# Attention handed to the scheduler: its hand-written order dropped, the first group's early matmuls at the lowest priority

## The chip, the core and the metric

One core of a Trainium2 chip runs the kernel. The metric is the time of one execution on the device in microseconds (us), the median of several runs. The engines are named as the profile names them: PE (matrix multiply, with PEld for its weight loads), DVE (vector), ACT (activation), POOL (GpSimd) and SP, which only issues transfers here. Each engine works through its own instructions strictly in the order in which they stand in the program; an instruction that waits for another engine holds up everything behind it on its own engine.

## The reference

```python
B, H, Sl, D = 4, 8, 512, 64;  Sg = 32;  window = 32;  scale = 1 / sqrt(D)
k_all, v_all = concat(k_g, k_l), concat(v_g, v_l)          # along the sequence
out_g = softmax(scale * q_g @ k_all.T) @ v_all             # 32 global queries see all
s_ll  = where(|i - j| <= window, scale * q_l @ k_l.T, -1e9)
s_l   = concat(scale * q_l @ k_g.T, s_ll)                  # local queries: globals and a band
out_l = softmax(s_l) @ v_all
x = concat(out_g, out_l) as 2176 tokens x 512
x = (silu(x @ w_gate) * (x @ w_val)) @ w_out               # 512 -> 1536 -> 512
y = mish(x @ w_in) @ w_out2                                # 512 -> 2048 -> 512
```

The seven arrays of the two feed-forward layers are wide numbers of 8 bytes, which the kernel turns into a high and a low 32-bit half itself.

## The kernel before

**Attention.** The 32 heads of the four batches are worked as 16 head pairs, numbered 0 to 15, four to a batch. `att_hp` is a head pair's work in seven steps: transpose keys and queries (`qkT`, L195); scores of the local rows in two halves (`sc`, L238, half 0 and half 1), each with a masked minimum on DVE (L243, four times) and an exponential on ACT (L247, four times); a reciprocal of the row sums (L226, L227 on DVE) and the multiplication with it on POOL (L228, L230); the transposes of the two halves (`pT`, L195) with a copy on ACT (L265); and the output (`o`, L272 and L276), which `split_to_x` writes as a high and a low half into the token tiles `x0` to `x4` (L137 on ACT, L138 on DVE). The halves' reciprocals are made by `normalise`: that of half 0 is written behind the scores of half 1.

`att_g` is the same for the 32 global queries, once for two head pairs: scores `ga` (L286), minimum on DVE (L294 to L296), exponential on ACT (L297), scaling on DVE (L303), transposes `gT` (L195), output `go` (L320). So a period of the attention is two head pairs with one `ga` in it.

**What goes on beside it.** The first group of the first feed-forward layer (two blocks f of 128 hidden columns) needs six weight blocks, `w0` to `w5`. `w_load` brings one with one transfer of 512 KB on SP's queue into one of three staging buffers `st`; `w_convert` turns it into two halves: a square on ACT (L408, `q<-st`), four operations on DVE (L410 to L414), a copy on ACT (L424), a subtraction on POOL (L425). A staging buffer is free for the next load when L414 is done.

`fill(t)` then works this group for a whole token tile: for both blocks 12 matmuls for `g` and 12 for `v` (L539; `g` and `v` each sum over four blocks kd of the tile, three matmuls each), the gate on ACT and DVE (L544 to L547), the high and low half (L473 on ACT, L459 on POOL), and 24 matmuls for the output (L560) with a copy on DVE (L562). That is 72 matmuls for a tile, and 216 for the three tiles 0, 1 and 2. They are called fill matmuls below. Tiles 3 and 4 of this group are worked behind the attention, as the first units of the dense stage (L448).

**What sets the order.** `attention()` gives every step a number, a place on a line on which head pair n begins at 10n; the steps are sorted by it and called. All of it runs under `tc.manual_schedule()`, so instructions stand on every engine in the order of the calls. The six conversions are at 16 to 48, one after about every 6; the fill of tile i is cut at each `yield` into 12 pieces (six matmuls in nearly all), at 44.9 + 40i onwards.

**The dense stage.** Behind the attention stand the units of all other groups, also in an order written by hand; that part is the same in both kernels. PSUM holds three double banks for attention (`ps_pair`) and two banks `ps_mm` for the fill.

Of the kernel before, what the change touches and what calls it, by code (L numbers as in the profile page):

```python
# [21 lines left out]
def tile_attn_moe_moe2(  # L22
# [73 lines left out]
    def setup():  # L96
        nc.gpsimd.memset(ident, 1.0)
        nc.gpsimd.affine_select(out=ident, in_=ident, pattern=[[-1, 128]], compare_op=ALU.is_equal,
                                fill=0.0, base=0, channel_multiplier=1)
        nc.vector.memset(qgbd, 0.0)  # L100
        for t in (vg, vgb):
            nc.vector.memset(t, 0.0)

        nc.gpsimd.memset(mask, 0.0)
        m = mask[:, 0:192]
        nc.gpsimd.affine_select(out=m, in_=m, pattern=[[1, 192]], compare_op=ALU.is_ge,
                                fill=NEG, base=0, channel_multiplier=-1)
        nc.gpsimd.affine_select(out=m, in_=m, pattern=[[-1, 192]], compare_op=ALU.is_ge,
                                fill=NEG, base=64, channel_multiplier=1)

        nc.gpsimd.tensor_copy(mask7, mask)
        nc.gpsimd.memset(mask7[64:96, 128:192], NEG)
        nc.gpsimd.memset(mask7[96:128, 64:128], NEG)
# [35 lines left out]
    def load_glob(b):  # L149
        gk = g_p.tile([128, 2, 128], F32, tag="gkq", name="gkq")  # L150
        for i, src in enumerate((k_g, q_g)):
            for h in range(2):
                (nc.sync if b else nc.scalar).dma_start(out=gk[:, i, 64 * h:64 * h + 64],
                                  in_=src[b].rearrange("(g h) p d -> h g p d", h=2)[h])
        GK[b] = gk

    def load_qk(b, hp):
        hs = slice(2 * hp, 2 * hp + 2)
        qs = qk_p.tile([128, 4, 2, D], F32, tag="qs", name="qs")
        ks = qk_p.tile([128, 4, 2, D], F32, tag="ks", name="ks")  # L160
        for h in range(2):
            nc.sync.dma_start(out=ks[:, :, h], in_=k_l[b, 2 * hp + h].rearrange("(c p) d -> p c d", p=128))
            nc.sync.dma_start(out=qs[:, 0:3, h],
                              in_=q_l[b, 2 * hp + h, SG:SG + 384, :].rearrange("(c p) d -> p c d", p=128))
        nc.sync.dma_start(out=qs[0:96, 3], in_=q_l[b, hs, SG + 384:SL, :].rearrange("h p d -> p h d"))
        nc.sync.dma_start(out=qs[96:128, 3], in_=q_l[b, hs, 0:SG, :].rearrange("h p d -> p h d"))
        QS[b, hp], KS[b, hp] = qs, ks

    def load_vg(b):

        for k in range(4):
            nc.sync.dma_start(out=vg[32 * k:32 * k + 32, k],
                              in_=v_g[b].rearrange("(g h) p d -> h p g d", h=2)[k % 2])

    def load_vgb(b):
        nc.sync.dma_start(out=vgb[96:128], in_=v_g[b].rearrange("h p d -> p h d"))

    def load_v(b, hp):

        hs = slice(2 * hp, 2 * hp + 2)  # L180
        vw = v_p.tile([128, NB, 2, D], F32, tag="vw", name="vw")
        for h in range(2):
            v = v_l[b, 2 * hp + h]
            windows = bass.AP(v.tensor, v.offset, [[D, 128], [64 * D, NB - 1], [1, D]])
            nc.sync.dma_start(out=vw[:, 0:NB - 1, h], in_=windows)
        nc.sync.dma_start(out=vw[0:64, NB - 1], in_=v_l[b, hs, SL - 64:SL, :].rearrange("h p d -> p h d"))
        nc.sync.dma_start(out=vw[64:128, NB - 1], in_=v_l[b, hs, 0:64, :].rearrange("h p d -> p h d"))
        VW[b, hp] = vw
# [151 lines left out]
    def load_at(i, load):  # L340
        if i < B * HP:
            load(i // HP, i % HP)

    def attention():


        steps = []

        def at(times, gen):
            for t in times:  # L350
                steps.append((t, lambda: next(gen)))

        for n in range(B * HP):
            b, hp = divmod(n, HP)
            t = 10 * n
            if hp == 0:
                steps.append((t - 6, lambda b=b: att_glob(b)))
                if b + 1 < B:
                    steps.append((t + 42.5, lambda b=b: load_vg(b + 1)))
                    steps.append((t + 38.7, lambda b=b: load_vgb(b + 1)))  # L360
            at((t - 4.5, t, t + 2.5, t + 5.8, t + 6.5, t + 9, t + 12), att_hp(b, hp))
            if n + 2 < B * HP:
                steps.append((t - 3, lambda n=n: load_at(n + 2, load_qk)))
                steps.append((t + (13 if hp % 2 else 18.5), lambda n=n: load_at(n + 2, load_v)))
            if hp % 2 == 1:
                at((t + 2.1, t + 4, t + 5, t + 8), att_g(b, hp // 2))
        steps.append((-0.5, lambda: load_v(0, 1)))
        steps += [(9.1, load_next), (9.2, load_next), (9.3, load_next)]
        for i, t in enumerate((16, 22, 28, 34, 41, 48)):
            at((t + 0.3, t + 1.8, t + 3.6), itertools.chain(w_convert(converts.pop(0)), iter([0])))  # L370
        for i, t in enumerate(FILL):
            at([44.9 + 40 * i + 10 * (k // 3) + 3 * (k % 3) + (1 if k % 3 == 2 else 0) for k in range(12)],
               itertools.chain(fill(t), iter([0])))
        for _, go in sorted(steps, key=lambda x: x[0]):
            go()

# [75 lines left out]
    def act_tile(tag, n):  # L452
        return act_p.tile([128, 512], F32, tag=tag, name=tag)[:, 0:n]
# [71 lines left out]
    def fill(t):  # L525

        n = TILES[t]
        fs = GROUPS[0][1]
        x = x_tile(t)
        aa = []  # L530
        for f in fs:
            s = act_tile("t", n)
            for kind in "gv":
                (wh, wl), (xh, xl) = W[0, f, kind], x
                p = ps_mm.tile([128, 512], F32, tag="mm", name=kind)[:, 0:n]
                for k in range(KD):
                    d = slice(128 * k, 128 * k + 128)
                    for j, (a, c) in enumerate(((wh, xh), (wh, xl), (wl, xh))):
                        nc.tensor.matmul(p, lhsT=a[:, d], rhs=c[:, k, :],  # L539
                                         start=(k == 0 and j == 0), stop=(k == KD - 1 and j == 2))  # L540
                    if k == 1:
                        yield
                if kind == "g":
                    nc.scalar.activation(out=s, in_=p, func=AF.Tanh, scale=0.5)  # L544
                    nc.vector.scalar_tensor_tensor(s, s, 1.0, p, op0=ALU.add, op1=ALU.mult)
                else:
                    nc.vector.scalar_tensor_tensor(s, s, 0.5, p, op0=ALU.mult, op1=ALU.mult)  # L547
                    a = hi_lo()
                    high(a, s, n)
                    a_low(a, s, n)  # L550
                    aa.append(a)
                yield
        ya = YA[t] = y_tile(t)
        for c in range(KD):
            d = slice(128 * c, 128 * c + 128)
            p = ps_mm.tile([128, 512], F32, tag="mm", name="mm")[:, 0:n]
            for f, (ah, al) in zip(fs, aa):
                wh, wl = W[0, f, "o"]
                for j, (l, r) in enumerate(((wh, ah), (wh, al), (wl, ah))):
                    nc.tensor.matmul(p, lhsT=l[:, d], rhs=r[:, 0:n], start=(f == fs[0] and j == 0),  # L560
                                     stop=(f == fs[-1] and j == 2))
            nc.vector.tensor_copy(ya[:, c * n:c * n + n], p)  # L562
            if c < KD - 1:
                yield

    def out_rows(c0, n):


        parts = [(b * SL + lo, hi - lo, b * S + r) for b in range(B)
                 for lo, hi, r in ((0, SL - SG, 2 * SG), (SL - SG, SL, SG))]  # L570
        parts += [(B * SL + b * SG, SG, b * S) for b in range(B)]
        for at, k, r in parts:
            a, e = max(c0, at), min(c0 + n, at + k)
            if a < e:
                yield a - c0, r + a - at, e - a
# [37 lines left out]
                nc.scalar.activation(out=yh[:, c, :], in_=ya, func=AF.Copy)  # L613
                nc.gpsimd.tensor_tensor(out=yl[:, c, :], in0=ya, in1=yh[:, c, :].bitcast(F32), op=ALU.subtract)

    with tc.manual_schedule():
        load_glob(0)
        load_qk(0, 0)
        setup()
        load_qk(0, 1)  # L620
        load_v(0, 0)
        load_vg(0)
        load_vgb(0)
        attention()
    early.close()
    ps_acc = pool("ps_acc", 4, space=PS)
    ps_at = pool("ps_at", 2, space=PS)
# [11 lines left out]
    with tc.manual_schedule():  # L639
# [12 lines left out]
        at = -1  # L652
        for n in range(6, len(order)):
            at = max(at + 1, last[order[n - 12]] - 1 if n >= 12 else 0, first[order[n]] - 14)
# [36 lines left out]
```

## Time and profile before

| what | value |
|---|---|
| median of 3 runs | 1036.7 us (1036.5 to 1036.8) |
| the profiled execution's own time | 1028.2 us |
| its span in the trace | 1026.1 us |
| PE busy | 951.0 us, 93% of the span |
| DVE, ACT, POOL busy | 584.9, 526.3, 364.5 us |

The span is the time from the first to the last instruction that the trace holds; the profiled execution took 2.1 us more than that, and 8.5 us less than the median. A busy PE is not always PE at full speed: the trace also has the clock that was granted to it.

### The profile page before, as it was taken

To read this page: it belongs to the slowest core of one execution; us is meant where nothing else is said; L and a number is where in the kernel's file an instruction comes from. 1 tells how busy PE (TensorE), PEld (TensorE's weight loads), DVE (VectorE), ACT (ScalarE), POOL (GpSimd) and SP (SyncE) were. 2 spreads that over 40 slices of the span, in tenths; PEclk is the share of its full clock that TensorE was granted. 3 is DMA by queue.
4 is the path that set the end of the run, shared out by engine and by line. 5 is a ranking of instruction groups with operands and counts; after the bars stand their busy time and mean duration, and the time that the engine had idled before them with its cause. 6 is when DMAs were issued, how large, how long until landed. Compare 5 with 4: busy or idle time off the path is not lost.

```text
span 1026.1 us, 15729 instructions
## 1 busy us (share of the span) xinstructions
PE 951.0 (93%) x6008; PEld 830.1 (81%) x6008; DVE 584.9 (57%) x1097; ACT 526.3 (51%) x1058; POOL 364.5 (36%) x353
## 2 busy tenths in 40 slices
PE   5577887887999999999999999999999999999998
PEld 4464676676889889899899898898789878988886
DVE  3666545554788884765755836374446735571223
ACT  3555545554323222222212234878687857877664
POOL 2434334323243342331422456433334423432222
PEclk8778988888999999999999999999999999999999
DMA  5634343320122220210211201021102100200112
GB/s 132 187 91 104 78 93 84 79 54 2 62 62 82 68 76 22 66 58 21 62 42 42 62 21 42 1 82 42 42 8 76 62 21 21 62 21 1 42 62 72
DMA packets 101386, 59.20 MB, mean 58 GB/s; under 512 B 75072, under 2 KB 95552, under 8 KB 101312
## 3 DMA queue, kind: packets, MB, share of 16 engines
q1 hardware_dynamic: 100784, 58.08, 20.3%
q8 instruction: 47, 0.77, 0.3%
q14 instruction: 27, 0.22, 0.1%
q10 hardware_dynamic: 528, 0.13, 0.1%
HBM read 53.74 MB, written 4.46 MB: 57 GB/s over the span
## 4 chain that ended last, share of the span: by engine, by line
PE 81%; DVE 10%; ACT 4%; POOL 3%; issue 1%; DMA 0%; ACTq 0%; DVEq 0%; POOLq 0%
PE acc L597 28%; PE h L448 16%; PE g L448 12%; PE v L448 12%; PE o L272 2%; DVE sm L243 2%; POOL sm L228 2%; PE sc L238 2%; PE o L276 2%; PE mm L560 2%; PE pT L195 1%; DVE sg L303 1%; DVE cx L412 1%; DVE cx L413 1%; PE g L539 1%
## 5 line engine op out<-in xcount | busy, mean ns | idle before, releaser
L459 POOL TENSOR_TENSOR al<-t,ah 128x384 fp32r<-128x384 f32 (+1 forms) x140 | 164.5, 1191 | 460.5 <-ACT ah L473 445.2
L473 ACT ACTIVATE ah<-t 128x384 fp32r<-128x384 f32 (+1 forms) x140 | 79.2, 566 | 154.9 <-DVE t L484 133.4
L513 DVE TENSOR_TENSOR t<-t,h 128x384 f32<-128x384 f32 (+1 forms) x80 | 47.1, 607 | 144.5 <-ACT t L512 144.2
L605 DVE TENSOR_TENSOR y<-acc,y 128x512 f32<-128x512 f32 (+1 forms) x151 | 92.6, 636 | 42.9 <-PE acc L597 42.2
L481 ACT ACTIVATE t<-g 128x384 f32<-128x384 f32 (+1 forms) x54 | 28.9, 536 | 133.5 <-PE g L448 132.4
L228 POOL TENSOR_TENSOR sm<-sm,rc 128x768 f32<-128x768 f32 x32 | 47.7, 1491 | 119.4 <-ACT sm L247 57.6
L413 DVE SCALAR_TENSOR_TENSOR cx<-fl,cx 128x512 uint32<-128x512 uint32 x68 | 79.4, 1168 | 2.3
L502 ACT ACTIVATE t<-h 128x384 f32<-128x384 f32 (+1 forms) x80 | 41.9, 523 | 59.8 <-PE h L448 59.6
L414 DVE SCALAR_TENSOR_TENSOR cx<-st,cx 128x512 uint32<-128x512 uint32 x68 | 69.1, 1017 | 2.3
L247 ACT ACTIVATE sm<-sm,nb 128x224 f32<-128x224 f32 x128 | 60.0, 471 | 20.4 <-DVE nb L243 20.4
L482 DVE SCALAR_TENSOR_TENSOR t<-t,g 128x384 f32<-128x384 f32 (+1 forms) x54 | 32.7, 605 | 56.9 <-ACT t L481 56.7
L410 DVE SCALAR_TENSOR_TENSOR fl<-q,st 128x512 f32<-128x512 f32 x68 | 60.0, 882 | 7.9 <-ACT q L408 7.9
L484 DVE SCALAR_TENSOR_TENSOR t<-t,v 128x384 f32<-128x384 f32 (+1 forms) x54 | 32.9, 608 | 47.2 <-PE v L448 45.9
L243 DVE CUSTOM_DVE_ANT_0 sm<-sc,mask 128x224 f32<-128x224 f32 x128 | 42.2, 386 | 22.2 <-PE sc L238 22.2
L503 ACT ACTIVATE t<-t,cst 128x384 f32<-128x384 f32 (+1 forms) x80 | 52.8, 660 | 2.6
L512 ACT ACTIVATE t<-t,cst 128x384 f32<-128x384 f32 (+1 forms) x80 | 49.4, 649 | 0.3
L412 DVE TENSOR_SCALAR cx<-fl 128x512 uint32<-128x512 uint32 x68 | 45.1, 663 | 6.0
L195 PE MATMUL pT<-ident,sm 64*128 64x64 f32 x256 | 18.7, 282 | 30.9 <-POOL sm L228 30.9
L408 ACT ACTIVATE q<-st 128x512 f32<-128x512 f32 x68 | 44.6, 655 | 0.0
L195 PEld LDWEIGHTS pT<-ident,sm 64*128 64x128 f32 x256 | 14.1, 180 | 36.0 <-POOL sm L228 34.3
L238 PE MATMUL sc<-kst,qT 64*128 64x224 f32 x256 | 39.5, 438 | 1.5 <-ACT qT L215 1.5
L512 ACT ACT_TABLE_LOAD x27 | 34.6, 1283 | 0.5
(899 smaller groups left out, 2864.2 us busy)
## 6 DMA issues: line engine op xcount, KB each, us to landing
st<-in_moe_w_out SPq DMA_DIRECT2D x28, 512.0 KB
st<-in_moe_w_in SPq DMA_DIRECT2D x16, 512.0 KB
vw<-in_v_l SPq DMA_DIRECT2D x32, 224.0 KB
st<-in_moe_w_gate SPq DMA_DIRECT2D x12, 512.0 KB
st<-in_moe_w_val SPq DMA_DIRECT2D x12, 512.0 KB
ks<-in_k_l SPq DMA_DIRECT2D x32, 128.0 KB
qs<-in_q_l SPq DMA_DIRECT2D x32, 96.0 KB
out<-y SPq DMA_DIRECT2D x12, 256.0 KB
```

The costliest lines, as they stand in the source:

```text
L228: nc.gpsimd.tensor_tensor(out=sm[:, i0:i1, 0:192], in0=sm[:, i0:i1, 0:192], in1=r.unsqueeze(2).to_broadcast([128, 4, 192]), op=ALU.mult)
L238: nc.tensor.matmul(p[:, h, 224 * pp:224 * pp + 224], lhsT=qT[half(h), 2 * g + pp, :], rhs=kst[half(h), 2 * g + pp, :], start=True, stop=True)
L243: nc.vector.tensor_tensor_reduce(out=sm[:, i], in0=p[:, h, 224 * pp:224 * pp + 224], in1=mask7 if 2 * g + pp == 3 else mask, scale=-scale, ...
L247: nc.scalar.activation(out=sm[:, i], in_=sm[:, i], func=AF.Exp, bias=nb_[:, i:i + 1], scale=-1.0, accum_out=su[:, i:i + 1])
L413: nc.vector.scalar_tensor_tensor(x, fu, 0xC0000000, x, op0=ALU.bitwise_and, op1=ALU.bitwise_or)
L414: nc.vector.scalar_tensor_tensor(x, st[:, :, 0], 29, x, op0=ALU.logical_shift_right, op1=ALU.bitwise_or)
L448: nc.tensor.matmul(p[:, 0:n], lhsT=a[:, d], rhs=c[:, k, :], start=(k == 0 and j == 0), stop=(k == KD - 1 and j == 2))
L459: nc.gpsimd.tensor_tensor(out=a[1][:, 0:n], in0=src, in1=a[0][:, 0:n].bitcast(F32), op=ALU.subtract)
L473: nc.scalar.activation(out=a[0][:, 0:n], in_=src, func=AF.Copy)
L512: nc.scalar.activation(out=s, in_=s, func=AF.Sin, scale=-2.0, bias=quarter)
L597: nc.tensor.matmul(p, lhsT=l, rhs=r, start=(first and j == 0), stop=(last and j == 2))
L605: nc.vector.tensor_tensor(out=ya, in0=p, in1=ya, op=ALU.add)
```

## The change

The attention is no longer called under `tc.manual_schedule()`. The sorted calls now give only a priority and the dependences: for each engine the compiler's scheduler takes, at each point of its own timeline, the instruction of the best priority that it holds to be ready, and may so move later work ahead of earlier work. The pieces of the fill are gone: `low_priority(t)` writes the whole fill of a tile in one go, at 52.5 + 36i, with a priority number that is a million worse than anything else in the attention. (All lines behind the edit have other numbers in the changed kernel, one less up to 7 more: L538 there is L539 before.)

```diff
         for i, t in enumerate(FILL):
-            at([44.9 + 40 * i + 10 * (k // 3) + 3 * (k % 3) + (1 if k % 3 == 2 else 0) for k in range(12)],
-               itertools.chain(fill(t), iter([0])))
+            steps.append((52.5 + 36 * i, lambda t=t: low_priority(t)))
...
+    def low_priority(t):
+        p = tc.cur_priority
+        tc.cur_priority = p + 1000000
+        for _ in fill(t):
+            pass
+        tc.cur_priority = p
...
-    with tc.manual_schedule():
-        load_glob(0)
...
-        attention()
+    load_glob(0)
...
+    attention()
```

**ACT, head pair 1.** The rows start with ACT's work behind the first copy of `pt` of head pair 0; `sm` is the exponential of the scores, `sg` that of `ga`, `q<-st` the first step of a weight's conversion, `w0h` its third. Before:

```order
L247 ACTIVATE sm,su<-sm,nb 128x224 x4
L137 ACTIVATE x0h<-o 128x512
L297 ACTIVATE sg,gsu<-ga,grc 128x512
L298 ACTIVATE sg,gsu<-ga,grc 128x32
L247 ACTIVATE sm,su<-sm,nb 128x224 x4
L312 ACTIVATE gtl<-gT 128x640
L215 ACTIVATE qT<-qkT 128x512
L408 ACTIVATE q<-st 128x512
```

In the changed kernel, at the same place:

```order
L247 ACTIVATE sm,su<-sm,nb 128x224
L407 ACTIVATE q<-st 128x512 x2
L297 ACTIVATE sg,gsu<-ga,grc 128x512
L298 ACTIVATE sg,gsu<-ga,grc 128x32
L423 ACTIVATE w0h<-cx 128x512
L137 ACTIVATE x0h<-o 128x512
L407 ACTIVATE q<-st 128x512
L423 ACTIVATE w1h<-cx 128x512
L407 ACTIVATE q<-st 128x512
L247 ACTIVATE sm,su<-sm,nb 128x224 x4
L312 ACTIVATE gtl<-gT 128x640
```

The first steps of four conversions now stand ahead of the four exponentials of half 1 of head pair 1, where none stood; all six conversions are over before the first exponential of head pair 2.

**PE, from `ga` to `gT` at head pairs 4 and 5.** `sc` is half 1 of head pair 5, the rows with `w1` or `w3` are fill matmuls of tile 0. Before:

```order
L286 MATMUL ga<-kst,qgbd 64x512 x2
L289 MATMUL ga<-kst,qgbd 64x32 x2
L238 MATMUL sc<-kst,qT 128x224 x4
L539 MATMUL v<-x0h,w1h 128x512
L539 MATMUL v<-x0l,w1h 128x512
L539 MATMUL v<-x0h,w1l 128x512
L539 MATMUL v<-x0h,w1h 128x512
L539 MATMUL v<-x0l,w1h 128x512
L539 MATMUL v<-x0h,w1l 128x512
L195 MATMUL gT<-ident,sg 128x64 x10
```

In the changed kernel, the end of the same stretch:

```order
L538 MATMUL v<-x0h,w3h 128x512
L538 MATMUL v<-x0l,w3h 128x512
L538 MATMUL v<-x0h,w3l 128x512
L195 MATMUL gT<-ident,sg 128x64 x10
L195 MATMUL qkT<-ident,ks 128x64 x8
L195 MATMUL qkT<-ident,qs 128x64 x8
```

Between `sc` and `gT` 24 fill matmuls stand now (the last three are shown), where six stood.

**DVE, half 0 of head pair 9.** The row sums' reciprocal is L226 with L227, `x2l` and `x3l` are the output's low halves of head pair 8. Before:

```order
L243 ISA nb 128x1
L138 TENSOR_TENSOR x2l<-o,x2h 128x256
L138 TENSOR_TENSOR x3l<-o,x3h 128x256
L294 TENSOR_REDUCE gmx<-ga 128x1
L295 TENSOR_REDUCE gmx<-ga 128x1
L296 TENSOR_TENSOR grc<-gmx 128x1
L243 ISA sm,nb<-sc,mask 128x224
```

In the changed kernel:

```order
L243 ISA nb 128x1
L226 TENSOR_SCALAR rc<-su 128x4
L227 RECIPROCAL rc<-rc 128x4
L138 TENSOR_TENSOR x2l<-o,x2h 128x256
L294 TENSOR_REDUCE gmx<-ga 128x1
L295 TENSOR_REDUCE gmx<-ga 128x1
L138 TENSOR_TENSOR x3l<-o,x3h 128x256
L296 TENSOR_TENSOR grc<-gmx 128x1
L243 ISA sm,nb<-sc,mask 128x224
```

The reciprocal of half 0 has moved ahead of the four minima (L243) of half 1; before, it stood behind the last of them.

## Rows read from the trace of the kernel before

**Rows 1.** The page: span, and busy time of the engines.
```profile
span 1026.1 us, 15729 instructions
PE 951.0 (93%) x6008; PEld 830.1 (81%) x6008; DVE 584.9 (57%) x1097; ACT 526.3 (51%) x1058; POOL 364.5 (36%) x353
```

**Rows 2.** Busy time by stretch: length, PE, PEld, DVE, ACT, POOL, clock, DMA, GB/s.
```profile
92.94:240.58 147.64, 121.45 (x1481) 97.18 (x1478) 78.07 (x291) 80.46 (x251) 50.96 (x76) 0.88 0.31 69
57.56:92.94 35.38, 25.08 (x284) 19.18 (x282) 24.00 (x67) 18.49 (x54) 15.29 (x18) 0.76 0.46 114
23.81:57.56 33.75, 20.15 (x264) 16.99 (x262) 22.17 (x63) 17.99 (x52) 13.49 (x16) 0.70 0.65 173
240.58:261.07 20.49, 16.16 (x171) 12.86 (x167) 8.22 (x29) 7.72 (x22) 3.85 (x4) 0.83 0.01 1
261.07:1026.10 765.03, 756.66 (x3708) 674.03 (x3708) 444.14 (x612) 392.09 (x651) 273.48 (x216) 1.00 0.15 47
```

**Rows 3.** PE's waits from 92.9 to 240.6: total us, times, longest.
```profile
PE gT L195 <- DVE sg L303: 14.5, 5, 3.1
PE pT L195 <- POOL sm L228: 11.7, 8, 2.1
```

**Rows 4.** Timeline of PE, one period: start, us; in brackets the wait.
```profile
144.31 0.46 PE L195 MATMUL pT<-ident,sm 64*128 64x64 f32 x8 [2.12 <-POOL sm L228]
...
152.25 1.03 PE L286 MATMUL ga<-kst,qgbd 128*64 128x512 f32 x4
153.11 0.26 PE L289 MATMUL ga<-kst,qgbd 128*64 128x32 f32 x4
153.29 1.03 PE L238 MATMUL sc<-kst,qT 64*128 64x224 f32 x8
154.25 0.44 PE L539 MATMUL v<-x1h,w1h 128*128 128x384 f32 x1
...
158.69 0.52 PE L195 MATMUL gT<-ident,sg 64*128 64x64 f32 x10 [3.12 <-DVE sg L303]
```

**Rows 5.** Timeline of ACT, head pairs 1 and 2.
```profile
23.07 0.47 ACT L247 ACTIVATE sm<-sm,nb 128x224 f32<-128x224 f32 x1
...
27.28 0.47 ACT L247 ACTIVATE sm<-sm,nb 128x224 f32<-128x224 f32 x1
...
32.87 0.66 ACT L408 ACTIVATE q<-st 128x512 f32<-128x512 f32 x1
...
37.72 0.48 ACT L247 ACTIVATE sm<-sm,nb 128x224 f32<-128x224 f32 x1 [0.22 <-DVE nb L243]
```

**Rows 6.** Timeline of SP: the first and the third of three weight loads.
```profile
26.10 0.43 SPq L397 DMA_DIRECT2D st<-in_moe_w_gate  x1
...
27.12 0.51 SPq L397 DMA_DIRECT2D st<-in_moe_w_gate  x1
```

**Rows 7.** The window in which those loads land (columns as in Rows 2).
```profile
28.00:32.00 4.00, 2.17 (x38) 2.09 (x38) 2.06 (x3) 1.94 (x7) 2.17 (x3) 0.71 1.06 368
```

**Rows 8.** Timeline of DVE and POOL: a weight's conversion, and work beside it.
```profile
33.56 1.28 DVE L410 SCALAR_TENSOR_TENSOR fl<-q,st 128x512 f32<-128x512 f32 x1 [0.99 <-ACT q L408]
34.88 0.51 DVE L412 TENSOR_SCALAR cx<-fl 128x512 uint32<-128x512 uint32 x1
36.14 0.69 DVE L414 SCALAR_TENSOR_TENSOR cx<-st,cx 128x512 uint32<-128x512 uint32 x1
...
78.02 1.47 POOL L228 TENSOR_TENSOR sm<-sm,rc 128x768 f32<-128x768 f32 x1 [5.88 <-ACT sm L247]
78.18 1.59 DVE L412 TENSOR_SCALAR cx<-fl 128x512 uint32<-128x512 uint32 x1
```

**Rows 9.** Timeline of PE: the two waits of head pair 2.
```profile
45.32 0.46 PE L195 MATMUL pT<-ident,sm 64*128 64x64 f32 x8 [3.42 <-POOL sm L228]
...
52.10 0.69 PE L195 MATMUL pT<-ident,sm 64*128 64x64 f32 x8 [5.97 <-POOL sm L228]
```

**Rows 10.** Timeline of PE: fill matmuls in step, at the higher and the lower clock.
```profile
101.23 0.40 PE L539 MATMUL g<-x0h,w2l 128*128 128x512 f32 x1
101.47 0.39 PE L539 MATMUL g<-x0h,w2h 128*128 128x512 f32 x1
...
115.72 0.63 PE L539 MATMUL v<-x0h,w3h 128*128 128x512 f32 x1
116.15 0.63 PE L539 MATMUL v<-x0l,w3h 128*128 128x512 f32 x1
```

More of the change, by code (lines that the diff above doesn't have):

```diff
@@ L614, in second @@
                 nc.gpsimd.tensor_tensor(out=yl[:, c, :], in0=ya, in1=yh[:, c, :].bitcast(F32), op=ALU.subtract)
-    with tc.manual_schedule():
-        load_glob(0)
[L618 to L623, printed above, removed]
-        attention()
+    load_glob(0)
+    load_qk(0, 0)
+    setup()
+    load_qk(0, 1)
+    load_v(0, 0)
+    load_vg(0)
+    load_vgb(0)
+    attention()
     early.close()
```

## The prediction, made before the result was known

> **What bounds the kernel now.** PE is busy for 951.0 of 1026.1 us [rows 1], so I read first where the other 75 lie. The table of busy time by stretch [rows 2] shows it. I cut it at the first matmul of `ga` of some periods (23.81, 57.56, 92.94, 240.58) and at 261.07, where the first `v` of the dense stage starts. Behind 261.07 PE is busy for 756.66 of 765.03 us at clock 1.00, and the order there is not touched: whatever the attention gains or loses moves that stage as a whole and reaches the end. [...]
>
> In the middle stretch (five periods, 29.5 us each) PE idles 147.64 - 121.45 = 26.2 us, and the list of waits names all of it: 14.5 us before `gT` and 11.7 us before `pT` [rows 3]. The timeline of one period shows why [rows 4]. From `ga` at 152.25 to `gT` at 158.69 runs a chain over DVE, ACT and DVE of 6.4 us; PE has `ga`, `sc` and six fill matmuls to put into it and then waits 3.12 us. Before `pT` it waits for POOL's multiplication, 2.12 us in the row shown. So the attention is bound by chains between the engines, and PE's fill stands partly in the gaps and partly beside them.
>
> **The change, stretch by stretch.** No instruction of the 216 fill matmuls, the conversions or the attention goes away; they move. I counted the fill in the new order of PE between the same `ga`: 12 ahead of the second `ga` (none before), 12 up to the third (18), 192 in the middle stretch (180), none behind (18). Six matmuls of the dense stage move from the last stretch to the middle one too.
>
> *First stretch (33.75 us).* The new order puts four conversions' squares on ACT ahead of the exponentials of half 1 of head pair 1. Their weights come late: the three loads are issued at 26.10 to 27.6 [rows 6], and in the window 28 to 32 the transfers move 368 GB/s [rows 7], 1.5 MB, about three loads of 0.5 MB. ACT is through with the exponentials of half 0 at 23.5 and then stands until the first load lands, at about 29.5 (an estimate from those rows; at the latest 32.87, when the old square found it there [rows 5]). The fourth load needs a staging buffer that the first conversion frees: 3.3 us of DVE (33.56 to 36.83 [rows 8]), so about 34, and 5 us for the load (the first three took 4 to 6 from issue). ACT reaches the four exponentials at about 40.5 instead of 27.28. Behind them stand the rest of four conversions, 4 x 3.3 = 13.2 us: the first exponential of head pair 2 comes at 53.7 instead of 37.72, 16 us late. Queued behind ACT's wait are `sg`, and with it `gT` and everything behind that on PE. From there it gets better: before, 37.72 to 57.56 took 19.84 us, of which PE waited 3.42 + 5.97 = 9.4 us [rows 9] for a POOL multiplication that stood behind the second conversion; those are over now. 53.7 + 10.4 = 64.1 against 57.56: **6.5 us lost**. Bounds: 5 gained (loads at once, so that only the waits go) to 14 lost (the 16 us keep).
>
> DVE's share of this depends on POOL. A row shows L412 at 0.51 us with POOL idle and at 1.59 us when it starts 0.16 us behind a POOL multiplication of 1.47 us [rows 8]. [...]
>
> *Second stretch (35.38 us).* Three conversions and six fill matmuls leave it. A period of the middle stretch, with no conversion and 36 fill matmuls, takes 29.5: the least gain is 5.9. With 24 fewer at 0.24 us [rows 10] it would be 23.8, but fewer fill brings waits for POOL back; nearer to the row that exists, I take 27.8: **7.6 gained** (5.9 to 11.6).
>
> *Middle stretch (147.64 us).* Two things touch its 26.2 us of waits. The fill between `ga` and `gT` is now 24, 6, 18, 6 and 18 matmuls instead of six each; 12 to 18 more at 0.18 to 0.24 us (the step between two of 512 columns [rows 10], and three quarters of it for 384) cover a wait of up to 3.1 us. So three of five `gT` waits go; the other two shrink, since part of `o` now stands behind `ga`: 2.6 left of 14.5. And the reciprocal of half 0 stands ahead of the minima of half 1, so POOL's multiplication starts earlier by their length and what stands between: the wait before the first `pT`, 2.12 us in the row [rows 4], goes. The one before the second `pT` stays, covered by 24 matmuls in two periods and 8 in one; where nothing stands there I expect 3.3 us (four exponentials at 0.47 [rows 5] and a multiplication at 1.47 [rows 8]), twice, and 0.9 (an estimate, a quarter of that) otherwise: 9.3 left of 11.7. PE's busy time grows by 18 matmuls, 3.4 us. 26.2 - 11.9 - 3.4 = **10.9 gained**. Bounds: nothing (each wait comes back at the next link) and 22.8 (all waits gone).
>
> *Last stretch (20.49 us).* 18 fill matmuls and six of the dense stage leave: at 0.18 to 0.32 each (three quarters of 0.24 and 0.43 [rows 10], for 384 columns) together 4.3 to 7.7 us of PE. Without them PE waits more for the last head pair's chain: I take **4.2 gained** (0 to 7.7).
>
> *Sum.* +6.5 - 7.6 - 10.9 - 4.2 = -16.2. The profiled execution took 1028.2, so 1012.0; it lay 8.5 under the median of 1036.7, and the same step on the median gives 1020.5. A difference below 0.2% (2 us) can't be told from none.
>
> **Rivals.**
> 1. *Slower: the runs lie on the chain.* [...] Of the 6.4 us from `ga` to `gT` only some 4.4 are free. Every period of the middle stretch has one run of 18 or 24, behind `ga` or between the two `pT`. If they run at the lower level, each puts `gT` or `pT` about 4 us late: 20 lost in place of the waits' 14.3, so 3.4 + 5.7 = 9 lost in place of 10.9 gained, and 1040.5. It decides once most runs meet the lower level. For it: the clock falls to 0.70 to 0.88 in attention, and 115.72 shows fill at the lower rate. Against: 101.23 shows it at the higher, and mean 0.88 is nearer to that.
> 2. *No change: the order does not matter.* The chain over ACT, DVE and POOL sets the period, and fill on PE is hidden in either order: the middle and last stretch give nothing, and the first two cancel: 1035.6. Against: these waits do have PE work that stands in the wrong place.
> 3. *Faster: the clock comes along.* Denser PE holds the higher clock: 121.45 x (1 - 0.88) = 14.6 us less in the middle stretch, 1006. For it: clock 1.00 wherever PE is busy without gaps [rows 2]. [...] The trace agrees on 0.88 with gaps and 1.00 without; but the first stretch gets a gap more.
>
> **How the numbers follow.** My forecast (1009 to 1028 around 1020.5, by the first stretch's bounds) 0.55; rival 3 0.15; rival 2 0.08; rival 1 0.15; and 0.07 for a first stretch worse than its bound with little gain behind. Slower has rival 1 and this 0.07: 0.22. Rival 2 lies at the edge of the 2 us, most of it counts as the same: 0.06. The rest, 0.72, is faster. The range that holds 8 in 10 reaches from 1004 (rival 3 and a bit) to 1040 (short of rival 1).
>
> **What would show it.** Right: a wait of ACT of 5 us or more before L407 near 24 us; the second `ga` near 64 and the third near 92; five periods of about 27.3; no `gT` wait behind the runs of 18 and 24; DVE's reciprocal right behind the minima; the dense stage's first `v` near 245 instead of 261.07 and unchanged behind it. Wrong: periods of 29 or more with `gT` starting straight behind a run, at a clock under 0.88 (rival 1); or the second `ga` past 72, if loads take longer than 5 us or conversions more than 3.3.

## The result, and the profile after

The changed kernel takes 1006.84 us (median; 1003.96 to 1007.69 in four executions) against 1036.72 us before (1036.5 to 1036.8), a ratio of 0.9707, 95% interval 0.9688 to 0.9727. That is 29.9 us less, where 16.2 were forecast: inside the range, on the predicted side, but nearly twice the size. Profile against profile (1006.5 against 1028.2) it is 21.7 us, and the 8.2 us between the two differences need a cause of their own (e1).

The page of the changed kernel, for [rows 1]:

```profile
span 1004.8 us, 15751 instructions
PE 944.4 (94%) x6008; PEld 822.3 (82%) x6008; DVE 571.8 (57%) x1097; ACT 523.8 (52%) x1058; POOL 362.0 (36%) x353
```

Busy time by stretch, for [rows 2], cut at the same instructions:

```profile
22.65:63.85 41.20, 26.55 (x272) 20.20 (x272) 29.20 (x75) 21.38 (x58) 18.78 (x20) 0.71 0.66 180
63.85:90.89 27.04, 22.56 (x312) 16.96 (x314) 13.43 (x57) 17.11 (x55) 10.07 (x15) 0.87 0.41 92
90.89:221.79 130.90, 114.48 (x1458) 92.29 (x1454) 69.81 (x293) 76.23 (x246) 49.46 (x75) 0.95 0.35 78
221.79:241.27 19.48, 14.79 (x180) 11.40 (x181) 6.30 (x25) 9.20 (x28) 3.65 (x4) 0.70 0.01 2
241.27:1004.80 763.53, 755.11 (x3708) 672.87 (x3708) 444.77 (x612) 392.05 (x651) 272.57 (x216) 1.00 0.15 47
```

The span is 21.3 us shorter: 1.2 less ahead of the first `ga`, 7.5 more in the first stretch, then 8.3, 16.7, 1.0 and 1.5 less. In the middle stretch PE idles 16.4 us instead of 26.2, and it is also busy 7.0 us *less*, at clock 0.95 instead of 0.88.

PE's waits in the middle stretch, the largest five, for [rows 3]:

```profile
PE pT L195 <- POOL sm L228: 7.0, 3, 3.4
PE g L538 <- DVE t L544: 3.4, 2, 1.7
PE mm L559 <- DVE y L561: 1.8, 2, 1.0
PE gkqT L329 <- ACT sg L298: 0.9, 1, 0.9
PE g L538 <- DVE x1l L138: 0.8, 1, 0.8
```

`gT` waits for `sg` no more. The first period's `gT` starts right behind a run of 24 fill matmuls, 2.8 us after DVE is done with `sg` (from the timelines of PE and DVE; the run's last row is shown):

```profile
90.89 1.03 PE L286 MATMUL ga<-kst,qgbd 128*64 128x512 f32 x4
...
95.29 0.50 DVE L303 TENSOR_SCALAR sg<-sg,grr 128x544 f32<-128x544 f32 x1
...
98.25 0.39 PE L538 MATMUL v<-x0h,w3l 128*128 128x512 f32 x1
98.57 0.53 PE L195 MATMUL gT<-ident,sg 64*128 64x64 f32 x10
```

The timeline of ACT, for [rows 5]: the wait for the first weight, half 1 of head pair 1, and the first exponential of head pair 2.

```profile
28.68 0.66 ACT L407 ACTIVATE q<-st 128x512 f32<-128x512 f32 x1 [4.43 <-DMA st<-in_moe_w_gate]
...
38.13 0.47 ACT L247 ACTIVATE sm<-sm,nb 128x224 f32<-128x224 f32 x1
...
53.58 0.47 ACT L247 ACTIVATE sm<-sm,nb 128x224 f32<-128x224 f32 x1
```

### The profile page after: what moved, and what is told of

Read it like the earlier page. It is cut to its first block, busy times and chain, and to the rows that moved or that the text cites. A ratio compares the mean times of both kernels' runs of the same rounds, so it can differ in the third digit from the quotient of the medians.

```text
span 1004.8 us, 15751 instructions
## 1 busy us (share of the span) xinstructions
PE 944.4 (94%) x6008; PEld 822.3 (82%) x6008; DVE 571.8 (57%) x1097; ACT 523.8 (52%) x1058; POOL 362.0 (36%) x353
## 4 chain that ended last, share of the span: by engine, by line
PE 80%; DVE 9%; ACT 7%; POOL 1%; issue 1%; DMA 1%; SPq 0%; DVEq 0%; ACTq 0%; POOLq 0%
PE acc L603 29%; PE h L447 16%; PE v L447 13%; PE g L447 13%; ACT sm L247 4%; PE sc L238 2%; DVE cx L412 1%; PE mm L559 1%; POOL sm L228 1%; PE g L538 1%; DVE fl L409 1%; PE v L538 1%; DVE sm L243 1%; PE pT L195 1%; DVE cx L411 1%
## 5 line engine op out<-in xcount | busy, mean ns | idle before, releaser
L412 DVE SCALAR_TENSOR_TENSOR cx<-fl,cx 128x512 uint32<-128x512 uint32 x68 | 81.6, 1200 | 2.2
L409 DVE SCALAR_TENSOR_TENSOR fl<-q,st 128x512 f32<-128x512 f32 x68 | 59.5, 875 | 9.6 <-ACT q L407 9.6
L243 DVE CUSTOM_DVE_ANT_0 sm<-sc,mask 128x224 f32<-128x224 f32 x128 | 42.2, 385 | 28.2 <-PE sc L238 28.2
L411 DVE TENSOR_SCALAR cx<-fl 128x512 uint32<-128x512 uint32 x68 | 43.8, 644 | 5.6
L195 PE MATMUL pT<-ident,sm 64*128 64x64 f32 x256 | 16.2, 252 | 18.9 <-POOL sm L228 18.3
```

The lines of the kernel that those rows point to most:

```text
L409: nc.vector.scalar_tensor_tensor(fl, q, TINY2, hw, op0=ALU.is_ge, op1=ALU.mult)
L412: nc.vector.scalar_tensor_tensor(x, fu, 0xC0000000, x, op0=ALU.bitwise_and, op1=ALU.bitwise_or)
```

## The experiments

The theory ahead of the runs was that of the prediction, order against waits, with rival 3 (the clock comes along) beside it, since PE's busy time had fallen. Each kernel was timed beside the kernel before on the same chip; a difference is against that.

**e1: the kernel before, again.** No edit.

> The kernel before, unchanged, to see the 8.5 us between its profiled execution (1028.2) and its timed ones (1036.5 to 1036.8). Theory A: executions of this order differ by the clock that is granted in the attention; then the profiled one comes out anywhere from 1028 to 1037, the clock in the records goes with the time, and the difference lies ahead of 261 us, in PE's busy time, not in its waits. Theory B: recording shortens this kernel by some 8 us each time; then it is 1028 again under the profile and 1036.5 timed, and the same step should be looked for in the changed kernel, where it was 0.

It took 1036.63 us (1030.71 to 1039.82, ten executions; 19 of before beside it: 1027.31 to 1039.79). The one under the profile took 1039.7. Theory A, though that lies above the 1037 that it named. The middle stretch of this profile, to be held against the first row of [rows 2]:

```profile
94.24:252.16 157.92, 130.44 (x1480) 104.68 (x1478) 78.05 (x291) 80.62 (x251) 51.08 (x76) 0.83 0.29 65
```

It is 10.3 us longer than in the profile that I predicted from. The waits are the same within 1.3 us (27.5 against 26.2); busy time is 9.0 us more, at 0.83 instead of 0.88. The same order has executions 12 us apart, most of it by the clock, and the profile read ahead of the prediction lay near the lower end of them. The rows of PE in one period show where the clock goes:

```profile
193.79 0.52 PE L195 MATMUL gT<-ident,sg 64*128 64x64 f32 x10 [2.90 <-DVE sg L303]
...
195.56 0.52 PE L560 MATMUL mm<-al,w4h 128*128 128x384 f32 x1
...
200.17 1.79 PE L238 MATMUL sc<-kst,qT 64*128 64x224 f32 x8
...
202.17 0.34 PE L560 MATMUL mm<-al,w4h 128*128 128x384 f32 x1
...
205.11 1.03 PE L238 MATMUL sc<-kst,qT 64*128 64x224 f32 x8
```

Behind a wait of 2.90 us everything takes longer for a while (`sc` 1.79 instead of 1.03 us, a fill matmul 0.52 instead of 0.34).

**e2: the scheduler alone.** The written order is given up; the fill keeps its twelve pieces and gets no priority.

```diff
-    with tc.manual_schedule():
-        load_glob(0)
...
-        attention()
+    load_glob(0)
...
+    attention()
```

> Only the written order is given up; the fill keeps its twelve pieces a tile at their old places in the program and gets no low priority. Theory A (the scheduler places the fill by when its operands are ready, and priority hardly decides): 1004 to 1009, the same as the changed kernel within 3 us, with runs of 18 and 24 fill matmuls in the same gaps. Theory B (the low priority is what moves the fill into the gaps): 1018 or more, with waits of gT of about 3 us back in each period.

1004.83 us (1003.7 to 1008.46), ratio 0.9729 (0.9658 to 0.9801): the changed kernel's time. Theory A; the second half of the change, the low priority, does nothing that can be measured.

**e6: the fill's half of the change alone.** The written order stays; a tile's 72 matmuls go in one block (the cut is against the kernel before).

```diff
-            at([44.9 + 40 * i + 10 * (k // 3) + 3 * (k % 3) + (1 if k % 3 == 2 else 0) for k in range(12)],
-               itertools.chain(fill(t), iter([0])))
+            steps.append((52.5 + 36 * i, lambda t=t: low_priority(t)))
```

> The other half of the change alone: the written order stays, and a tile's 72 fill matmuls stand in one block at 52.5, 88.5 and 124.5. Theory A (all the gain is the scheduler's, which takes the block apart): a block is 17 us at the higher clock, with waits for its own conversions inside it, three times across the attention's chain; periods without fill wait 4 to 5 us before gT; 1050 to 1075. Theory B (it is enough that the fill stands together and keeps PE dense): 1010 to 1025.

1057.43 us (1057.37 to 1058.65), ratio 1.0205 (1.019 to 1.022). Theory A: the five periods take 183.99 us. The changed kernel's gain comes with the scheduler's order, not with the block.

**e3: the first three periods by hand.** The changed kernel, steps below 52.4 in the written order.

```diff
+    with tc.manual_schedule():
...
+        for t, go in steps:
+            if t < 52.4:
+                go()
+    for t, go in steps:
+        if t >= 52.4:
+            go()
```

> The changed kernel, but all steps up to 52.4 of the old list (three periods, with the six conversions at their old places) keep the written order; the rest is the scheduler's. Theory A (the first stretch was lost because ACT stands before the first conversion's weights, with the exponentials behind it): the wait of ACT before 28.7 goes, the second ga is back at 57 to 58.5 instead of 63.85, and the third stays near 89 to 91, because three conversions come back into the second stretch and take 2 to 4 us of the 6; the total is 1001 to 1005. Theory B (the conversions cost the same wherever they stand): the third ga at 92 or later and 1006 to 1010.

1006.23 us (1004.56 to 1007.9), ratio 0.9734 (0.9675 to 0.9792): theory B. The first two stretches:

```profile
23.48:55.29 31.81, 22.88 (x277) 17.96 (x274) 22.17 (x63) 17.05 (x50) 13.49 (x16) 0.73 0.65 172
55.29:92.67 37.38, 29.32 (x302) 23.38 (x300) 27.22 (x70) 20.00 (x57) 17.20 (x19) 0.77 0.46 118
```

ACT's wait is gone and the second `ga` is 8.6 us earlier than in the changed kernel, but the third comes at 92.67, after 90.89 there. The 69.2 us of both stretches are 68.2 in the changed kernel: what it loses in the first it gets back in the second, since the conversions are then over.

**e4: more fill between `ga` and `gT`, in the written order.**

```diff
-            at([44.9 + 40 * i + 10 * (k // 3) + 3 * (k % 3) + (1 if k % 3 == 2 else 0) for k in range(12)],
+            at([44.9 + 40 * i + 20 * (k // 6) + (3, 9.9, 9.95, 10, 17, 19)[k % 6] for k in range(12)],
```

> The written order of before, with only the fill moved: in each period 18 fill matmuls instead of 6 between sc behind ga and gT, six each at three other places. Theory A (the waits before gT come from too little fill there): the waits before gT in the five periods from 92 fall from 14.5 to under 3 us, those before pT grow by no more than 3, and the time is 1022 to 1030. Theory B (the chain over ACT, DVE and POOL sets the period, so that a wait only moves on): the waits before pT grow by 10 or more, 1034 to 1039. Theory C (a run of 18 at the low clock takes 7.7 us and pushes gT back): over 1040.

1041.09 us (1034.42 to 1042.63), ratio 1.0059 (1.0028 to 1.0089). The waits of its five periods:

```profile
PE pT L195 <- POOL sm L228: 17.4, 12, 2.1
PE mm L560 <- ACT ah L473: 8.0, 2, 4.1
PE go L320 <- ACT gtl L312: 3.4, 3, 1.3
PE gT L195 <- DVE sg L303: 2.5, 2, 1.5
```

12 of 14.5 us before `gT` went, and came back before `pT` (13.0 in e1), before `mm` (which now follows the last `v` at once and waits for its own operand) and before `go`, where the fill had stood. That is theory B in kind, but not in size: it named 10 us more before `pT` and 1039 at most. The time is theory C's, and some of C is there: in two of the five periods the fill ran at the lower level behind the waits of 3.9 and 4.1 us before `mm` (0.63 us a matmul of 512 columns, 0.52 of 384), and `gT` came behind it, at 135.61 and 198.24, 13.9 and 12.6 us behind its `ga`, where a `gT` that waits for `sg` (162.05) comes 6.9 us behind. So the step that the prediction gave most words to, fill as cover, doesn't explain the gain by itself.

**e5: the reciprocal's place alone.** The written order, `normalise(0)` ahead of the minima of half 1.

```diff
         for g in range(2):
...
+            if g:
+                normalise(0)
             for pp in range(2):
...
-            if g:
-                normalise(0)
             yield
```

> The written order of before, with one thing moved: the normalisation of half 0 is issued behind the scores of half 1 and ahead of their minima, as the scheduler puts it. Theory A (the waits before the first pT come from the reciprocal's place on DVE): those of the five periods fall from 12 to 13 us to 4 or less, nothing comes back elsewhere, and the time is 5 to 9 us under before's 1036.6. Theory B (DVE now stands until the exponentials of half 0 are through, with the minima of half 1 behind it, and so the second pT gets what the first gave up): waits of pT the same in sum within 3 us, 1034 to 1040.

1006.43 us (1005.78 to 1006.92), ratio 0.9708 (0.9692 to 0.9724): 30.5 us, all of the change's gain, by moving two DVE instructions a head pair (and with them the POOL work that they release). Theory A gave the place, but 5 to 9 us for it. The middle stretch and its waits:

```profile
90.23:223.30 133.07, 114.16 (x1480) 91.36 (x1478) 70.88 (x291) 80.18 (x251) 50.14 (x77) 0.95 0.34 77
...
PE gT L195 <- DVE sg L303: 10.5, 5, 2.3
PE pT L195 <- POOL sm L228: 8.4, 11, 0.9
```

Waits fall from 27.5 (e1) to 18.9 us, the longest from 3.1 to 2.3, and busy time from 130.44 to 114.16. Of 24.9 us two thirds (16.3) are busy time, at clock 0.95 instead of 0.83. `gT` gains too, though nothing was moved there. In the kernel before, in the period of [rows 4], POOL's multiplication and DVE's of `sg` meet:

```profile
156.52 0.13 DVE L301 SCALAR_TENSOR_TENSOR grr<-gsu 128x1 f32<-128x1 f32 x1
...
156.78 1.47 POOL L228 TENSOR_TENSOR sm<-sm,rc 128x768 f32<-128x768 f32 x1 [9.68 <-ACT sm L247]
...
156.88 1.66 DVE L303 TENSOR_SCALAR sg<-sg,grr 128x544 f32<-128x544 f32 x1
```

In e5 they don't:

```profile
145.76 1.47 POOL L228 TENSOR_TENSOR sm<-sm,rc 128x768 f32<-128x768 f32 x1 [7.48 <-DVE rc L227]
...
145.79 0.39 DVE L245 CUSTOM_DVE_ANT_0 sm<-sc,mask 128x224 f32<-128x224 f32 x1
...
146.72 0.52 DVE L301 SCALAR_TENSOR_TENSOR grr<-gsu 128x1 f32<-128x1 f32 x1
147.27 0.16 DVE L302 RECIPROCAL grr<-grr 128x1 f32<-128x1 f32 x1
147.47 0.50 DVE L303 TENSOR_SCALAR sg<-sg,grr 128x544 f32<-128x544 f32 x1
```

L303 takes 1.66 us beside POOL and 0.50 behind it, and L301, the one to wait now, takes 0.52 instead of 0.13. All eight L303 of the kernel before take 1.63 to 1.66 us, all eight of the changed kernel 0.49 to 0.50. PE's rows show the clock behind a `gT` that waits (a fill matmul of 384 columns takes 0.34 us at the higher level):

```profile
148.12 0.52 PE L195 MATMUL gT<-ident,sg 64*128 64x64 f32 x10 [2.32 <-DVE sg L303]
...
149.87 0.52 PE L539 MATMUL g<-x1l,w2h 128*128 128x384 f32 x1
```

In three of the five periods the lower level follows that wait (2.32, 2.10 and 2.32 us), in the other two (1.97 and 1.76 us) it doesn't.

**e7: useless matmuls where PE waits.** The kernel before, with matmuls added that write into banks which the transposes then overwrite.

```diff
+    def warm(p, n):
+        for _ in range(n):
+            nc.tensor.matmul(p[:, 0, 0:224], lhsT=ident, rhs=mask, start=True, stop=True)
...
         p = bank("gT")
+        if True:
+            warm(p, 8)
...
             p = bank("pT")
+            if g == 0 and hp % 2 == 0 and (b or hp):
+                warm(p, 5)
```

> The kernel before, in its written order, with useless work added where PE waits: 8 matmuls of the mask against the unit matrix (224 columns, some 0.37 us each at the higher clock, an estimate from gkqT's 128 columns) ahead of each gT and 5 ahead of the first pT of each even head pair, into the bank that the transposes then overwrite. Theory A (the waits cost twice, once as idle time and again by the lower clock behind them): the granted clock of the five periods rises from 0.83 to 0.88 to 0.95 or more, their busy time without the added matmuls falls by 10 us or more, and the time falls, though work was added: 1015 to 1028. Theory B (the waits are only idle time, and the clock goes its own way): the added matmuls change nothing at the higher clock, 1035 to 1040, and cost 10 us or more where they run at the lower one, 1046 or more.

1016.66 us (1016.21 to 1016.89), ratio 0.9808 (0.9794 to 0.9823): 20 us faster, with more work. Theory A. The middle stretch, and the added matmuls in it (each stands in two rows):

```profile
92.98:232.04 139.06, 134.70 (x1610) 110.43 (x1608) 77.97 (x291) 80.75 (x251) 51.01 (x77) 1.00 0.33 74
...
L199 PE MATMUL gT<-mask,ident 128*128 128x224 f32 x80 | 16.2, 355 | 0.6 <-ACT sg L304 0.5
L199 PE MATMUL pT<-mask,ident 128*128 128x224 f32 x50 | 10.8, 363 | 0.0
```

Without the added 27.0 us PE is busy 107.7 us, against 130.44 in e1 for the same work. The clock is 1.00 throughout, and the executions lie within 0.7 us of each other instead of 12.

**e8: the same in the first three periods of e3.** `warm` ahead of two `gT` and of two first `pT`.

> The kernel with the first three periods in the written order and the rest left to the scheduler (e3), with the same useless matmuls in those three periods alone: 8 ahead of the two gT, 5 ahead of the first pT of head pairs 2 and 4. Theory A (the clock of 0.73 to 0.77 there comes from the gaps): the clock of the two stretches rises to 0.90 or more, together they take 61 to 65 us instead of 69.2, and the time is 998 to 1003. Theory B (these stretches are set by the conversions on DVE, 49 of 69 us busy, and by the weights' loads): 68 us or more, 1005 to 1010.

1010.51 us (1009.63 to 1011.95), ratio 0.9751 (0.9735 to 0.9766). The clock rose as theory A said (0.89 and 0.86 in the two stretches, from 0.73 and 0.77), the time did not fall as it said: 31.83 and 37.79 us, 69.6 together. Theory B: there the clock isn't what bounds. The whole came out 4 us over e3; of the 3.4 us between the two profiles 1.9 lie in the five periods (130.45 us at 0.91, 128.53 at 0.95), which were not edited.

**e10: e5, with useless matmuls ahead of `gT`.** `warm(p, 6)`, nowhere else.

> e5 with 6 useless matmuls ahead of each gT (0.36 us each in e7, 2.1 us in all, where e5 still waits 2.1 to 2.3 us). Theory A (a wait of some 2 us still lowers the clock behind it): the clock of the five periods rises from 0.95 to 1.00 and the time falls by the 4 to 6 us of busy time that this gives back: 1000 to 1003. Theory B (what is left of the low clock there comes from elsewhere): 1005 to 1008, the added matmuls hidden.

1005.55 us (1002.11 to 1006.93), ratio 0.9728 (0.9653 to 0.9802), not told apart from e5. The five periods take 132.52 us at 0.97: theory B by the time. The rows are half theory A's. No `gT` has the lower level behind it now; without the added 12.4 us PE is busy 110.7 us, against 114.16 in e5. But six useless matmuls take 2.5 us and not the 2.1 expected (0.36 is the mean of one row, and each stands in two), 12.4 in place of 10.5 us of waits, which takes back most of it. What is left of the lower level stands behind short waits before a second `pT`, in two periods, as here:

```profile
165.72 0.69 PE L195 MATMUL pT<-ident,sm 64*128 64x64 f32 x8 [0.84 <-POOL sm L232]
...
166.31 1.80 PE L242 MATMUL sc<-kst,qT 64*128 64x224 f32 x8
```

**e9: e5, with `ga` ahead of the `o` before it.**

```diff
-                at((t + 2.1, t + 4, t + 5, t + 8), att_g(b, hp // 2))
+                at((t + 1.9, t + 4, t + 5, t + 8), att_g(b, hp // 2))
```

> e5 (written order, reciprocal of half 0 ahead of the minima of half 1) with one number more changed: att_g's first step at t + 1.9 instead of t + 2.1, so that ga stands ahead of the o of the head pair before it, and o's 2 us lie between ga and gT. Theory A (what is left before gT in e5, 10.5 us in the five periods, is PE work in the wrong place): those waits fall under 3 us, the clock reaches 0.97 or more, and the time is 996 to 1002, under both kernels. Theory B (the wait moves on to pT, or o comes late for the banks and the rows of x): waits of pT grow by as much, 1004 to 1009.

1009.4 us (1007.25 to 1012.26), ratio 0.9776 (0.9712 to 0.9841). Neither theory: nothing moved to `pT`, the waits before `gT` just stayed (2.36 us in the row below). From `ga` to `gT` are 8.95 us now, 5.64 in e5. DVE's and PE's timelines say why:

```profile
139.91 1.08 PE L286 MATMUL ga<-kst,qgbd 128*64 128x512 f32 x4
...
144.74 0.42 DVE L138 TENSOR_TENSOR x2l<-o,x2h 128x256 fp32r<-128x256 f32 x1 [2.37 <-ACT x2h L137]
...
148.21 0.50 DVE L303 TENSOR_SCALAR sg<-sg,grr 128x544 f32<-128x544 f32 x1
...
148.86 0.53 PE L195 MATMUL gT<-ident,sg 64*128 64x64 f32 x10 [2.36 <-DVE sg L303]
```

On DVE, `sg`'s last step stands behind the two subtractions on `o` and the minima of the next scores: its sums were there at 143.51 (ACT's L298), and L301, which reads them, began at 147.46. What I moved behind `ga` on PE went ahead of `sg` on DVE, and `gT` later by as much.

**e11: e5, with the fill moved too.** 18 matmuls between `ga` and `gT`, six behind the first `pT`.

```diff
-            at([44.9 + 40 * i + 10 * (k // 3) + 3 * (k % 3) + (1 if k % 3 == 2 else 0) for k in range(12)],
+            at([44.9 + 40 * i + 20 * (k // 6) + (0, 3, 9.9, 9.95, 10, 13)[k % 6] for k in range(12)],
```

> e5 (written order, reciprocal of half 0 ahead of the minima of half 1) with the fill's pieces moved: 18 matmuls between ga and gT, six behind the first pT, six ahead of qkT and six between the two pT of the next head pair, none ahead of the two o. Unlike e4, the piece behind pT stays, and the first pieces of mm no longer follow the last v at once. Theory A (what is left in e5 is 10.5 us before gT and the clock behind them): gT's waits fall under 3 us, the five periods take 118 to 126 us at a clock of 0.98 or more instead of 133.07 at 0.95, and the time is 991 to 999, under both kernels. Theory B (the chain over ACT and DVE sets the period, so that the waits come back before pT, o or mm): 1002 to 1008.

995.51 us (995.42 to 996.58), ratio 0.9611 (0.9573 to 0.9649): theory A, and 11 us under the changed kernel. Its five periods and their longest waits:

```profile
86.72:210.81 124.09, 107.27 (x1480) 87.14 (x1478) 70.39 (x290) 78.81 (x251) 51.35 (x77) 1.00 0.37 86
...
PE pT L195 <- POOL sm L228: 10.6, 13, 1.3
PE mm L560 <- DVE y L562: 4.0, 2, 2.2
PE gT L195 <- DVE sg L303: 1.4, 2, 0.7
```

With the reciprocal early, fill as cover works: 9.1 us less before `gT`, 2.2 more before `pT`, 4.0 before `mm`, and the clock at 1.00.

**e12: the change without its early reciprocal.**

```diff
-            nc.vector.tensor_scalar(r, su[:, i0:i1], 1e-9, None, op0=ALU.add)
+            if g == 0:
+                nc.vector.scalar_tensor_tensor(r, nb_[:, 4:8], 0.0, su[:, i0:i1], op0=ALU.mult, op1=ALU.add)
+            else:
+                nc.vector.tensor_scalar(r, su[:, i0:i1], 1e-9, None, op0=ALU.add)
```

> The changed kernel, with the reciprocal of half 0 bound to the minima of half 1 (it adds 0 times their columns in place of 1e-9), so that no order can put it ahead of them; the scheduler orders everything else as it finds best. Theory A (the reciprocal's place is what the change gains by; the fill's place is worth little): most of the gain goes, 1025 to 1040. Theory B (the scheduler's placement of the fill covers the later multiplication on POOL as well): 1005 to 1013, with more fill ahead of pT. In between, both carry it.

1024.45 us (1022.06 to 1025.23), ratio 0.9882 (0.9834 to 0.9931): in between; 17 of the 30 us are gone. Its five periods:

```profile
95.98:238.93 142.95, 121.56 (x1449) 99.78 (x1446) 73.78 (x293) 77.53 (x246) 49.50 (x75) 0.87 0.32 71
...
PE pT L195 <- POOL sm L231: 16.0, 7, 3.8
```

The scheduler covered `gT` in its own way (1.8 us left, none of it for `sg`), and the step that was L303 takes 0.49 us in the mean of its six places behind 90 us, where it took 1.66 in the kernel before. But `pT` waits 16.0 us instead of 7.0, up to 3.8 at a time, and the clock is back at 0.87. Of the 18.2 us between this profile and the changed kernel's 12.1 lie in the five periods.

## Why the prediction was right, and where not

*First and second stretch: right, in part by luck.* Second `ga` forecast at 64.1, measured at 63.85, from a first one 1.2 us earlier than before: 7.5 us lost, not 6.5. ACT's wait for the first weight ends at 28.68 (forecast 29.5; 4.43 us long, where the sign asked for 5), the first exponential of head pair 2 comes at 53.58 (53.7). Between these two lie errors that cancel: half 1 of head pair 1 came at 38.13 and not 40.5, and from there it took 15.4 us and not 13.2. DVE was held up 3.8 us in four conversion steps that began while POOL worked (L409 1.95 us, elsewhere 0.69; L411 1.11 and 1.34, elsewhere 0.42 to 0.55; L412 1.64, elsewhere 0.69 to 0.71 but for 1.65 at 33.65, also beside POOL), for which the prediction's 4 x 3.3 us have no term. Its row of L412 "with POOL idle" is misread: POOL's L230 ran from 34.25 to 35.10 there. The second stretch gained 8.3 us (7.6). The two are one account, as rival 2 had it ("the first two cancel"): e3 undid the loss and lost the gain.

*Middle stretch: the mis-sized term.* "PE's busy time grows by 18 matmuls, 3.4 us" took the clock as given. Busy time fell by 7.0 us. Some of it is no gain: at the end of the stretch most of an `o` (about 1.5 us) went over into the next one, which is part of why the last stretch gained 1.0 us and not 4.2 (its clock, too, was 0.70 instead of 0.83). The rest came with the clock, 0.95 instead of 0.88: rival 3's case, to which I had given 0.15 by itself. It belonged in the forecast: against e1 (27.5 us idle in the five periods, 0.83) the clock was higher in e5 (18.9, 0.95), e11 (16.8, 1.00) and e7 (4.4, 1.00), if not in step with the idle time (e12: 21.4, 0.87; the kernel before in its first profile: 26.2, 0.88). The term for the waits was nearer: 9.8 us gained against 14.3 forecast. `gT` waits 0 us for `sg` (2.6 left forecast) and `pT` 7.0 (9.3; the two of 3.3 us came at 3.25 and 3.36). But 6.4 us of waits are new, all of the fill: 5.2 for one of its two PSUM banks, which DVE had still to read (`t`, `y`), and 1.2 for `x`. Packed runs bring them, and I had not counted them. Rival 3's figure of 1006 is the measured time, but by luck: it put 14.6 us of clock on top of the forecast, where busy time fell by 7.0 and the rest came from which execution of before had been profiled.

*The cause behind the `gT` waits: half right.* I counted on fill as cover. e4 shows that fill moved in this way by hand gains nothing while the reciprocal is late, and e5 that the reciprocal alone gains as much as the whole change. That the totals agree is partly chance: against e1's profile the changed kernel gains 27.0 us in the middle stretch, 1.3 in the first two and 1.0 in the last, e5 24.9, 3.3 and 3.7 (that profile lies 3 us above the median). And without the early reciprocal the scheduler's order still gains 12.8 us (e12). So the two overlap, and no run splits the 29.9 us between them. I had the reciprocal right as the end of one wait before `pT`, and missed two things that it does. It takes POOL's multiplication out of the way of L303, 1.66 to 0.50 us, on the very chain from `ga` to `gT` that I had timed at 6.4 us; L301 gives back 0.39 of this, and the 0.8 us that are left come, in five periods, to nearly all of the 4.0 us by which the `gT` waits fell from e1 to e5. I weighed POOL's work against the conversions alone and left the two rows shown in e5 (156.78 and 156.88) unread on the critical chain. And it makes the waits shorter, 18.9 instead of 27.5 us, with the clock at 0.95 instead of 0.83 (e5 against e1).

*The clock's price: shown by e7.* Covering the waits with matmuls that compute nothing gave 20 us: in the five periods PE idled 4.4 us instead of 27.5, and the work of before was busy 107.7 us at clock 1.00 instead of 130.44 at 0.83 (e1). In the rows of e1 a wait of 2.9 us is followed by some 7 us (195 to 202) at the lower level. The length of a wait doesn't settle which one costs: e5 has the lower level behind three of its five `gT` waits, e10 behind waits of 0.84 and 0.83 us, and e11 has 1.00 with one of 2.2. So a wait of the kernel before can cost twice, and the clock of rival 3 belonged in the forecast (121.45 us in [rows 2] less 107.7 is 13.8, near its 14.6). Why one execution of before falls back more often than another stays open.

*"The same step on the median": wrong.* The 8.5 us between the profiled execution and the median are not a constant beside the kernel. They are nearly all clock in the attention (e1: 9.0 of 10.3 us), which the change takes away as well: its own profile lies at its median. From e1's profile, 3 us above the median where the first lay 8.5 under it, the middle stretch gives 157.92 - 130.90 = 27.0 us.

*Rivals 1 and 2.* The runs of 18 and 24 did reach the chain, but cost PE no wait: `sg` was done 1.2 to 2.8 us before the three runs ahead of `gT` ended. They ran at the higher level (0.39 us a row in the one shown) but for ten matmuls of one between two `pT`; rival 1 needed most of them at the lower. Its "about 4 us late" is an estimate: 18 or 24 matmuls at the step from 115.72 to 116.15 in [rows 10], 0.43 us, are 7.7 or 10.3 us, against some 4.4 that are free. None of the changed kernel's runs of 18 and 24 was at the lower level throughout: these ten, at 0.52 us each, are all. That order does not matter is refuted by e5 and e6, 51 us apart with the same instructions.

*Low priority.* Its part is nothing that can be measured (e2: 1004.83 us without it, 1006.84 with it); the forecast did not ask for it apart from the scheduler's order.

## What to carry to other kernels

Before costing a wait on TensorE at its length, look at the durations of the same matmul behind it; if they grow, as `sc` does from 1.03 to 1.79 us behind 2.90 us of waiting (e1), the wait costs twice, and it is to be cut first, by whatever work there is (20 us in e7). Look on every queue for a small instruction that releases another engine's long one and stands behind work that it doesn't need: here two instructions on DVE, moved past four minima, were worth as much as the whole scheduler (30.5 and 29.9 us). Moving PE work to cover a wait helps only if no other engine's queue has the moved work's consumers ahead of the chain (in e9 `gT` still waited 2.36 us), and if the work's own operands are ready there (in e4 `mm` waited 8.0 us for them).

## What was not expected of the hardware

One order of instructions on one core took from 1027.3 to 1039.8 us (e1). e5, e7 and e11 stayed within 1.2 us, but e10, whose waits are shorter than e5's, spread over 4.8; what decides it is open. DVE's minima, which read their scores from PSUM, kept their 0.36 to 0.39 us while POOL multiplied beside them (e5, 145.5 to 147), where L301 (0.52 us there, 0.13 in the kernel before) and L303 (1.66 in the kernel before, 0.50 in e5), on SBUF alone, did not; no run tells whether that is why. The dense stage, untouched, took 763.4 to 763.5 us in some profiles (the changed kernel, e4, e10, e11) and 765.0 to 765.4 in others (the kernel before, e1, e3, e5 to e9, e12); no run tells why.
